# Tails of the first two batches at other places among the loads and last in the kv sums, loads of later batches behind the q transpositions

## The chip, the cores and the metric

The kernel runs on one NeuronCore of a Trainium2 chip. The metric is the device time of one execution in microseconds (us), as the median of several runs. The engines are TensorE (PE, with its weight loads shown apart as PEld), VectorE (DVE), ScalarE (ACT), GpSimd (POOL) and SyncE (SP), which issues nearly all DMAs of this kernel on one queue.

## The reference

Attention with linear cost, followed by a feed-forward layer. All inputs and the output are float32; 8 batches, 8 heads, 576 positions, head dimension 64.

```python
theta = pi / 2 * arange(S) / S
phi(x) = concat([max(x, 0) * cos(theta), max(x, 0) * sin(theta)], axis=-1)   # 64 -> 128 features
q_p, k_p = phi(q), phi(k)
kv  = einsum('bhsf,bhsd->bhfd', k_p, v)
z   = sum(k_p, axis=s)
num = einsum('bhsf,bhfd->bhsd', q_p, kv)
den = einsum('bhsf,bhf->bhs', q_p, z) + 1e-6
x   = (num / den) as [4608, 512]          # rows: batch and position, columns: head and dimension
h   = x @ w_in                            # 512 -> 2048
out = max(0.01 * h, h) @ w_out            # 2048 -> 512
```

## The kernel before

**Tiling.** The 576 positions of a batch are 512 "main" positions (four tiles j = 0 to 3 of 128) and a tail of 64. The tails of two heads share one 128-row tile, so a batch's k tail (`kpt`, four weights of 128 x 128) covers all its heads; each of the k and v tails is loaded in two DMAs of 64 KB with rows of 256 bytes (`load_kvtail`, L91). The main part of q, k or v of a batch is 1 MB with rows of 1 KB (`load_main`, L81), as one DMA or as two halves of four heads. The q tails of all batches form a ninth group of 512 rows at the end. Groups 0 to 7 are the batches, group 8 is the tails.

**Steps of a batch.** DVE (in part ACT) builds `kpm` and `kpt` from k (`k_main`, L236, two instructions for one tile j, a cosine and a sine half; `k_tail`, L243). v is cast to float16 into `vmain` and `vtail` (`v_main`, `v_tail`; on POOL from batch 4 on). `kv_mm` (L256) sums k by v over all positions into PSUM: for each pair of heads one tail matmul of 132 columns, which opens the sum, and then eight main matmuls of 66 columns. Two of the columns are ones, so that z comes with kv. `q_prep` (L294) builds `qp`, again two DVE instructions for one tile; it is transposed on PE (`q_transpose`, batches 0 and 1) or by DMA (`q_transpose_dma`, L302). `num` (L328) multiplies it by kv and `divide` (L342) gives x, which is transposed too. `ffn1` (L402) and `ffn2` (L421) are the feed-forward layer: 64 matmuls of 512 columns each for one group.

**Order.** The schedule is manual: every engine takes its instructions in the order in which the program emits them, and waits in that order. The first two batches are written out by hand. For the others the matmuls of ffn1 of group g+1 and ffn2 of group g are woven into a list of units with positions (16 positions for one group), and each of the other steps has a position at which it is emitted (`weave`, L546; `load_steps`, `kv_steps`, `q_steps`, `out_steps`). For the same position, the order of the calls decides. `q_steps(b, start, step, lag)` emits the preparation of tile j at `start + j * step` and its transposition by DMA at `lag` behind it; `load_steps(b, pk, pv, pq)` gives the positions of the loads of k, of v (each with its tail) and of q. SP's queue takes loads, transpositions by DMA and the stores of `out` in one order.

**Buffers.** All 1 MB loads use a pool of seven `stage` buffers in turn, the tails of k and v one of four. PSUM has two buffers for ffn1, two for ffn2 and one for kv sums and num.

**The start.** Loads stand in this order before: q of batch 0 in two halves, the tails of k and v, then first half of k, first half of v, second halves; then w_in in eight pieces. Behind them: w_out pieces 0 and 1, q of batch 1, tails of batch 1, w_out pieces 2 and 3, halves of k and v of batch 1, and then batch 2. Dummy matmuls (`idle`, L159) fill PE's time while it waits for the first loads.

Of the kernel before, what the change touches and what calls it, by code (L numbers as in the profile page):

```python
# [14 lines left out]
J = 4  # L15
# [3 lines left out]
def kernel(  # L19
# [14 lines left out]
    nc = tc.nc  # L34
# [11 lines left out]
    NE = D + 2  # L46
# [25 lines left out]
    def psum(where, shape, dtype, name):  # L72
        p = {"h": ps_h, "o": ps_o, "n": ps_n}[where]
        return p.tile(shape, dtype, name=name, tag="ps_" + where)

    st = {}
    ACT, DVE, POOL = nc.scalar, nc.vector, nc.gpsimd
# [3 lines left out]
    def load_main(nm, src, b, parts=(0, 1)):  # L81

        if parts[0] == 0:
            st[nm, b] = stage.tile([P, H, J, D], dt.float32, name=f"{nm}st", tag="stage")
        lo, hi = 4 * parts[0], 4 * parts[-1] + 4
        nc.sync.dma_start(  # L86
            st[nm, b][:, lo:hi],
            src[b, lo:hi, 0:MAIN, :].rearrange("h (p j) d -> p h j d", j=J),
        )

    def load_kvtail(nm, src, b):  # L91

        t = kvtail.tile([P, H // 2, D], dt.float32, name=f"{nm}tl", tag="kvtail")
        v4 = src[b, :, MAIN:S, :].rearrange("(c o) p d -> o p c d", o=2)
        for o in range(2):
            nc.sync.dma_start(t[o * TAIL : (o + 1) * TAIL], v4[o])  # L96
        st[nm + "t", b] = t
# [18 lines left out]
    def load_halves(b):  # L116
        for hg in range(2):
            load_main("k", k, b, (hg,))
            load_main("v", v, b, (hg,))
# [20 lines left out]
    def load_w2(i):  # L140
        t = stage.tile([P, 4, DM], dt.float32, name="w2st", tag="stage")
        nc.sync.dma_start(t, w2v[i])
        st["w2", i] = t

    load_main("q", q, 0, (0,))
    load_main("q", q, 0, (1,))
    load_kvtail("k", k, 0)
    load_kvtail("v", v, 0)
    load_halves(0)
    for i in range(NB):  # L150
        for cp in range(2):
            load_w1(i, cp)
# [6 lines left out]
    def idle(n):  # L159
        ps = psum("o", [P, MAIN], dt.float32, "ps_idle")  # L160
        for _ in range(n):
            nc.tensor.matmul(ps, lhsT=blank[:, 0:P], rhs=blank)  # L162
# [18 lines left out]
        base=0,  # L181
# [3 lines left out]
    for o in range(2):  # L185
# [3 lines left out]
            base=MAIN,  # L189
# [12 lines left out]
    vmain, vtail = [], []  # L202
# [15 lines left out]
    def phi_half(eng, o, i, col):  # L218
        if eng is ACT:
            nc.scalar.activation(o, i, AF.Relu, scale=col)  # L220
        else:
            eng.tensor_scalar(  # L222
                out=o, in0=i, scalar1=0.0, scalar2=col, op0=ALU.max, op1=ALU.mult
            )
# [7 lines left out]
    def kp_tiles(b):  # L232
        st["kpm", b] = kppool.tile([P, H, J, F], dt.float16, name="kpm")
        st["kpt", b] = kppool.tile([P, H // 2, F], dt.float16, name="kpt")

    def k_main(b, j, eng_c, eng_s, lo=0, hi=H):  # L236
        kpm, kst = st["kpm", b], st["k", b]
        for eng, t, f in ((eng_c, cos_t, 0), (eng_s, sin_t, D)):
            phi_half(
                eng, kpm[:, lo:hi, j, f : f + D], kst[:, lo:hi, j, :], t[:, j : j + 1]  # L240
            )

    def k_tail(b, eng_c, eng_s):  # L243
        kpt, kt, c = st["kpt", b], st["kt", b], J
        phi_half(eng_c, kpt[:, :, 0:D], kt, cos_t[:, c : c + 1])
        phi_half(eng_s, kpt[:, :, D:F], kt, sin_t[:, c : c + 1])

    def v_main(b, lo, hi, eng):
        copy(eng, vmain[b % 2][:, lo:hi, :, 0:D], st["v", b][:, lo:hi])

    def v_tail(b, eng):
        for o in range(2):
            sl = slice(o * TAIL, (o + 1) * TAIL)
            copy(eng, vtail[b % 2][sl, :, o, 0:D], st["vt", b][sl])

    def kv_mm(b, hg, ps):  # L256
        kpm, kpt = st["kpm", b], st["kpt", b]
        for cc in range(2):
            c = 2 * hg + cc
            nc.tensor.matmul(  # L260
                ps[:, 2 * cc * NE : 2 * (cc + 1) * NE],
                lhsT=kpt[:, c, :],
                rhs=vtail[b % 2][:, c].rearrange("p a e -> p (a e)"),
                start=True,
                stop=False,
            )
            for o in range(2):
                h = 2 * c + o
                for j in range(J):
                    nc.tensor.matmul(  # L270
                        ps[:, (2 * cc + o) * NE : (2 * cc + o + 1) * NE],
                        lhsT=kpm[:, h, j, :],
                        rhs=vmain[b % 2][:, h, j, :],
                        start=False,
                        stop=(o == 1 and j == J - 1),
                    )

    def kv_all(b):
        ps = psum("n", [P, 2, 512], dt.float32, "ps_kv")[:, :, 0 : 4 * NE]
        for hg in range(2):  # L280
            kv_mm(b, hg, ps[:, hg])
        nc.scalar.copy(kv[b].rearrange("p (a h) e -> p a (h e)", a=2), ps)

    def kv_half(b, hg, where):
        ps = psum(where, [P, 4 * NE], dt.float32, "ps_kvh")
        kv_mm(b, hg, ps)
        nc.scalar.copy(kv[b][:, 4 * hg : 4 * hg + 4].rearrange("p h e -> p (h e)"), ps)
# [201 lines left out]
    for j in range(J):  # L489
# [2 lines left out]
        q_transpose(0, j, ACT)  # L492
        idle(1)
    kp_tiles(0)
    k_tail(0, DVE, DVE)
    v_tail(0, DVE)
    for j in range(J):
        k_main(0, j, DVE, DVE, 0, 4)
    v_main(0, 0, 4, ACT)
    for j in range(2):  # L500
        k_main(0, j, ACT, DVE, 4, 8)
# [29 lines left out]
    for m in range(4):  # L531
        ffn1(0, m, half, MAIN, range(2, 4))

    for i in range(2):
        load_w2(i)
    load_main("q", q, 1)
    load_kvtail("k", k, 1)
    load_kvtail("v", v, 1)
    for i in range(2, 4):
        load_w2(i)  # L540
    load_halves(1)
# [21 lines left out]
    def at(pos, f, *args):  # L563
        steps.append((pos, lambda: f(*args)))
# [16 lines left out]
    ps = psum("n", [P, 2, DM], dt.float32, "ps_o")  # L581
# [27 lines left out]
    ps = psum("n", [P, 2, MAIN], dt.float16, "ps_x")  # L609
# [41 lines left out]
    def load_steps(b, pk, pv, pq):  # L651
        at(pk, load_k, b)
        at(pv, load_v, b)
        at(pq, load_main, "q", q, b)

    def out_steps(b, start, step, lag):
        for j in range(J):
            at(start + j * step, num, b, j)
            at(start + j * step + lag, x_transpose_dma, b, j)

    def q_steps(b, start, step, lag):
        for j in range(J):
            at(start + j * step, q_prep, b, j)
            at(start + j * step + lag, q_transpose_dma, b, j)
# [9 lines left out]
    kv_steps(3, 20, 0.7, 24, ACT)  # L674
    out_steps(3, 24.5, 1.4, 1)

    load_steps(4, 20.5, 22.5, 19)
    kv_steps(4, 28, 1.2, 34, POOL)
    q_steps(4, 30, 1, 0.8)
    out_steps(4, 36.8, 2, 1.6)  # L680

    for b in range(5, NG):
        base = 16 * (b - 2)
        if b < B:
            load_steps(b, base - 14.5, base - 13, base - 17)
            kv_steps(b, base - 9.5, 1.4, base - 2, POOL)
        else:
            for j in range(J):
                at(base - 11.5 + 2 * j, load_qtail, j)
        q_steps(b, base - 8, 2, 1)  # L690
        out_steps(b, base + 1, 2, 1.6)
# [32 lines left out]
```

## Time and profile before

| | |
|---|---|
| median of 3 runs | 296.37 us (295.9 to 296.65) |
| the profiled execution | 297.1 us, of which the span from the first to the last instruction is 295.0 us |
| granted TensorE clock | 1.000 |
| PE busy | 286.8 us (97%), 1932 matmuls |
| DVE busy | 132.9 us (45%) |
| ACT busy | 107.8 us (37%) |
| POOL busy | 24.0 us (8%) |
| DMA | 56.93 MB, 88773 packets, of them 56880 under 512 bytes; mean 193 GB/s |
| chain that ended last | PE 80%, DMA 13%, SP's queue 3%, ACT 1% |

Times in the profile are us from the span's start. Matmuls overlap in the records: one of 512 columns is shown with 0.38 us and the next one starts 0.216 us behind it. A bracket at the end of a timeline's row gives how long the engine was idle before it and what ended that. "Chain" is the work that ended last, followed back from the last instruction to whatever released it at each step. The state of a queue is not shown as such: what a DMA waits for is read from its issue by SP, and from the first instruction that uses what it loads.

### The profile page before, as it was taken

How to read it: one execution, taken by the hardware profiler on the slowest of the kernel's cores; microseconds unless marked ns; L12 is line 12 of the kernel's file. 1: busy time of each engine (PE TensorE's matmuls, PEld its weight loads, DVE VectorE, ACT ScalarE, POOL GpSimd, SP SyncE). 2: the span in 40 equal slices, each digit the busy share in tenths (PEclk: the TensorE clock that was granted, in tenths of full speed). 3: DMA queues.
4: the chain of work that ended last, by engine and by line, in shares of the span. 5: the costliest groups of instructions: out<-in, count | busy, mean ns of one | idle time of the engine just before them, and what ended most of it. 6: DMA issues, size and time to landing. Idle time of an engine off the chain costs nothing.

```text
span 295.0 us, 4811 instructions
## 1 busy us (share of the span) xinstructions
PE 286.8 (97%) x1932; PEld 153.9 (52%) x1932; DVE 132.9 (45%) x328; ACT 107.8 (37%) x128; POOL 24.0 (8%) x36
## 2 busy tenths in 40 slices
PE   8799999999999999999999999999999999999995
PEld 3575556465455455555545554555445544444444
DVE  6950578934855925933572347333323211000011
ACT  4846376664253422242223222322222232222200
POOL 2055000000000400400300021000000000000000
PEclk9999999999999999999999999999999999999999
DMA  7999999999999999999978995416681210011132
GB/s 219 355 386 406 290 350 346 329 170 333 186 269 285 205 248 265 267 158 315 241 143 230 216 234 126 110 53 144 143 159 56 71 53 38 36 43 61 41 71 71
DMA packets 88773, 56.93 MB, mean 193 GB/s; under 512 B 56880, under 2 KB 81712, under 8 KB 88240
## 3 DMA queue, kind: packets, MB, share of 16 engines
q1 hardware_dynamic: 88672, 56.57, 75.7%
q8 instruction: 15, 0.25, 0.4%
q14 instruction: 6, 0.05, 0.1%
q10 hardware_dynamic: 80, 0.07, 0.1%
HBM read 36.70 MB, written 9.44 MB: 156 GB/s over the span
## 4 chain that ended last, share of the span: by engine, by line
PE 80%; DMA 13%; SPq 3%; ACT 1%; issue 0%; DVE 0%; POOL 0%
PE ps_h L411 37%; PE ps_o L430 37%; DMA ktl<-in_k_dram 5%; DMA w1st<-in_moe_w_in_dram 4%; DMA vst<-in_v_dram 3%; PE ps_num L333 3%; PE ps_kv L270 2%; SPq L86 2%; SPq L96 1%; SPq L138 1%; DMA out_dram<-osb 1%; PE ps_kv L260 0%; ACT xT L389 0%; ACT g L419 0%; ACT xT L612 0%
## 5 line engine op out<-in xcount | busy, mean ns | idle before, releaser
L411 PE MATMUL ps_h<-xT,w 128*128 128x512 f16 (+1 forms) x592 | 143.1, 373 | 0.6 <-ACT g L419 0.2
L430 PE MATMUL ps_o<-w,g 128*128 128x512 f16 x560 | 139.4, 379 | 0.0
L419 ACT ACTIVATE g<-ps_h 128x1024 f16<-128x1024 f32 x72 | 73.5, 1024 | 141.7 <-PE ps_h L411 141.6
L411 PEld LDWEIGHTS <-w 128*128 128x128 f16 x592 | 64.3, 114 | 53.6 <-issue 1.3
L430 PEld LDWEIGHTS <-g 128*128 128x128 f16 x560 | 54.1, 98 | 61.6 <-issue 0.2
L230 DVE COPY osb<-ps_o 128x512 f32<-128x512 f32 x33 | 22.7, 690 | 76.6 <-PE ps_o L430 76.6
L344 DVE TENSOR_SCALAR den<-ps_num 128x8 f32<-128x8 f32 x28 | 4.6, 166 | 54.1 <-PE ps_num L333 54.1
L230 POOL CAST vmain<-vst 128x1024 f16<-128x1024 f32 (+1 forms) x9 | 9.8, 1107 | 136.6 <-DMA vst<-in_v_dram 136.6
L349 DVE TENSOR_TENSOR xs<-ps_num,rden 128x512 f16<-128x512 f32 x28 | 19.4, 691 | 1.0
L222 DVE TENSOR_SCALAR kpm<-kst,sin_t 128x512 f16<-128x512 f32 (+1 forms) x40 | 18.3, 472 | 0.7 <-DMA kst<-in_k_dram 0.7
L222 DVE TENSOR_SCALAR qp<-qst,cos_t 128x512 f16<-128x512 f32 (+1 forms) x34 | 16.3, 479 | 3.8 <-DMA qst<-in_q_dram 3.8
L222 DVE TENSOR_SCALAR qp<-qst,sin_t 128x512 f16<-128x512 f32 (+1 forms) x34 | 16.1, 472 | 0.0
L333 PEld LDWEIGHTS <-qpT 128*128 128x128 f16 (+1 forms) x256 | 11.2, 101 | 7.3 <-issue 1.9
L222 DVE TENSOR_SCALAR kpm<-kst,cos_t 128x512 f16<-128x512 f32 (+1 forms) x29 | 14.1, 485 | 0.1
L333 PE MATMUL ps_num<-kv,qpT 128*128 128x66 f16 (+1 forms) x256 | 12.4, 194 | 0.0
L270 PEld LDWEIGHTS <-kpm 128*128 128x128 f16 x256 | 10.6, 97 | 2.8 <-DVE kpm L222 0.7
L162 PE MATMUL ps_idle<-blank 128*128 128x512 f16 x28 | 9.2, 467 | 1.2 <-DVE blank L157 1.2
L228 ACT COPY qpT<-ps_qt 128x1024 f16<-128x1024 f16 x8 | 7.8, 1019 | 7.0 <-PE ps_qt L323 7.0
L230 DVE CAST w<-w2st 128x2048 f16<-128x2048 f32 x4 | 4.9, 1227 | 11.7 <-DMA w2st<-in_moe_w_out_dram 11.7
L230 POOL CAST w<-w1st 128x1024 f16<-128x1024 f32 x8 | 8.3, 1042 | 16.4 <-DMA w1st<-in_moe_w_in_dram 16.4
L270 PE MATMUL ps_kv<-vmain,kpm 128*128 128x66 f16 x192 | 8.1, 193 | 0.0
L348 DVE RECIPROCAL rden<-den 128x8 f32<-128x8 f32 x36 | 7.3, 203 | 1.2
(57 smaller groups left out, 102.6 us busy)
## 6 DMA issues: line engine op xcount, KB each, us to landing
out_dram<-osb SPq DMA_DIRECT2D x32, 256.0 KB, 2.7
qst<-in_q_dram SPq DMA_DIRECT2D x7, 1024.0 KB, 8.0
kst<-in_k_dram SPq DMA_DIRECT2D x6, 1024.0 KB, 7.9
vst<-in_v_dram SPq DMA_DIRECT2D x6, 1024.0 KB, 8.3
w1st<-in_moe_w_in_dram SPq DMA_DIRECT2D x8, 512.0 KB, 12.1
w2st<-in_moe_w_out_dram SPq DMA_DIRECT2D x4, 1024.0 KB, 11.3
kst<-in_k_dram SPq DMA_DIRECT2D x4, 512.0 KB, 8.2
vst<-in_v_dram SPq DMA_DIRECT2D x4, 512.0 KB, 8.6
```

What stands on the lines that cost most here:

```text
L86: nc.sync.dma_start(st[nm, b][:, lo:hi], src[b, lo:hi, 0:MAIN, :].rearrange("h (p j) d -> p h j d", j=J),)
L162: nc.tensor.matmul(ps, lhsT=blank[:, 0:P], rhs=blank)
L222: eng.tensor_scalar(out=o, in0=i, scalar1=0.0, scalar2=col, op0=ALU.max, op1=ALU.mult)
L228: nc.scalar.copy(o, i)
L230: eng.tensor_copy(o, i)
L270: nc.tensor.matmul(ps[:, (2 * cc + o) * NE : (2 * cc + o + 1) * NE], lhsT=kpm[:, h, j, :], rhs=vmain[b % 2][:, h, j, :], start=False, stop ...
L333: nc.tensor.matmul(ps[lo:hi, h // 4, (h % 4) * NE : (h % 4 + 1) * NE], lhsT=qpT[:, h, lo:hi], rhs=kv[b][:, h, :],)
L348: nc.vector.reciprocal(rden, den)
L349: nc.vector.tensor_tensor(out=xs, in0=ps[:, :, 0 : 4 * NE].rearrange("p a (b e) -> p a b e", e=NE)[:, :, :, 0:D], in1=rden.rearrange("p (a ...
L411: nc.tensor.matmul(ps[:, m % 2, lo:hi], lhsT=w1[m // 4][c // 2][:, c % 2, m % 4 : 512 : 4], rhs=xT[:, c, lo:hi], start=(c == 0 and lo == 0 ...
L419: nc.scalar.activation(st["g", g][:, m - 1 : m + 1, :], ps, AF.Lrelu)
L430: nc.tensor.matmul(ps, lhsT=st["g", g][:, m, tt * P : (tt + 1) * P], rhs=w2[:, m, :], start=(m == 0), stop=(m == NFT - 1),)
```

## The change

Five edits, none of which adds or removes an instruction:

1. In the loads of batch 0 the four tail DMAs go behind the first halves of k and v. On DVE the k tail and v tail of batch 0 go behind the four pieces of the first half of k.
2. In `kv_mm` the tail matmul comes last for each pair of heads and closes the sum, and the first main matmul opens it.
3. In the loads of batch 1 the k tail goes between w_out pieces 0 and 1 and the v tail behind piece 1, both ahead of q.
4. For batch 4, the load of q moves from position 19 to 21.3 and the load of k from 20.5 to 21.4, behind the transpositions of q of batch 3 (18.8 to 21.2). The step of `q_steps(4, ...)` goes from 1 to 0.8, which puts the preparations at 30, 30.8, 31.6 and 32.4 and the transpositions at 30.8 to 33.2. The k pieces of that batch stay at 29.2, 30.4, 31.6 and 32.8.
5. For batches 5 to 7, the load of q moves from `base - 17` to `base - 14.6`, 0.1 ahead of the load of k.

```diff
     load_main("q", q, 0, (0,))
     load_main("q", q, 0, (1,))
+    load_main("k", k, 0, (0,))
+    load_main("v", v, 0, (0,))
     load_kvtail("k", k, 0)
     load_kvtail("v", v, 0)
-    load_halves(0)
+    load_main("k", k, 0, (1,))
+    load_main("v", v, 0, (1,))
...
         for cc in range(2):
             c = 2 * hg + cc
-            nc.tensor.matmul(
-                ps[:, 2 * cc * NE : 2 * (cc + 1) * NE],
-                lhsT=kpt[:, c, :],
-                rhs=vtail[b % 2][:, c].rearrange("p a e -> p (a e)"),
-                start=True,
-                stop=False,
-            )
             for o in range(2):
...
                         rhs=vmain[b % 2][:, h, j, :],
-                        start=False,
-                        stop=(o == 1 and j == J - 1),
+                        start=(o == 0 and j == 0),
+                        stop=False,
                     )
+            nc.tensor.matmul(
+                ps[:, 2 * cc * NE : 2 * (cc + 1) * NE],
+                lhsT=kpt[:, c, :],
+                rhs=vtail[b % 2][:, c].rearrange("p a e -> p (a e)"),
+                start=False,
+                stop=True,
+            )
...
     kp_tiles(0)
+    for j in range(J):
+        k_main(0, j, DVE, DVE, 0, 4)
     k_tail(0, DVE, DVE)
     v_tail(0, DVE)
-    for j in range(J):
-        k_main(0, j, DVE, DVE, 0, 4)
     v_main(0, 0, 4, ACT)
...
-    for i in range(2):
-        load_w2(i)
+    load_w2(0)
+    load_kvtail("k", k, 1)
+    load_w2(1)
+    load_kvtail("v", v, 1)
     load_main("q", q, 1)
-    load_kvtail("k", k, 1)
-    load_kvtail("v", v, 1)
     for i in range(2, 4):
         load_w2(i)
     load_halves(1)
...
-    load_steps(4, 20.5, 22.5, 19)
+    load_steps(4, 21.4, 22.5, 21.3)
     kv_steps(4, 28, 1.2, 34, POOL)
-    q_steps(4, 30, 1, 0.8)
+    q_steps(4, 30, 0.8, 0.8)
     out_steps(4, 36.8, 2, 1.6)
...
-            load_steps(b, base - 14.5, base - 13, base - 17)
+            load_steps(b, base - 14.5, base - 13, base - 14.6)
```

## The prediction

> **What bounds the kernel now.** I read the page first, then busy time by stage, then the chain of waits, then the timelines of single engines around the steps that move. The page's row of TensorE (40 slices of 7.4 us) is full but for its ends:
> ```profile
> PE   8799999999999999999999999999999999999995
> ```
> Busy time by stage (first column the stage, then its length, then PE busy with the count) makes it exact: from 60 to 281 us PE is busy 221.00 of 221.00 us.
> ```profile
> 0.00:60.00 60.00, 55.42 (x437) 32.28 (x438) 40.25 (x114) 36.62 (x52) 11.01 (x20) 1.00 1.02 331
> 60.00:281.00 221.00, 221.00 (x1434) 115.54 (x1433) 90.14 (x211) 70.85 (x76) 13.02 (x16) 1.00 0.72 163
> ```
> So what moves after 60 us cannot gain; it can only open a hole. Before 60 us DMA is the bound (share 1.02). The chain runs through the loads there and reaches PE by the second half of v of batch 1 (start, length, what):
> ```profile
> 37.26 10.15 DMA vst<-in_v_dram
> ...
> 48.13 0.58 PE ps_kvh L270 x8
> ```
> PE's timeline shows where it waits for loads and where it does not:
> ```profile
> 36.48 0.61 PE L323 MATMUL ps_qt<-ident,qp 128*128 128x128 f16 x8
> ...
> 44.40 0.22 PE L260 MATMUL ps_kvh<-vtail,kpt 128*128 128x132 f16 x1
> 44.90 0.41 PE L270 MATMUL ps_kvh<-vmain,kpm 128*128 128x66 f16 x8 [0.28 <-DVE vmain L230]
> ...
> 47.70 0.22 PE L260 MATMUL ps_kvh<-vtail,kpt 128*128 128x132 f16 x1
> 48.13 0.58 PE L270 MATMUL ps_kvh<-vmain,kpm 128*128 128x66 f16 x8 [0.21 <-POOL vmain L230]
> ```
> The tail matmul is through in 0.06 us (in the chain), so PE loses 0.44 us at 44.46 and 0.37 us at 47.76, with 0.17 us more among the matmuls behind: 0.98 us in all. This is what batch 1 can give.
>
> Last, the sums of batch 4 (DVE's timeline, then PE's):
> ```profile
> 97.55 1.26 DVE L222 TENSOR_SCALAR kpm<-kst,cos_t 128x512 f16<-128x512 f32 x1
> 98.73 1.25 DVE L222 TENSOR_SCALAR kpm<-kst,sin_t 128x512 f16<-128x512 f32 x1
> ...
> 102.96 0.48 DVE L222 TENSOR_SCALAR kpm<-kst,sin_t 128x512 f16<-128x512 f32 x1
> 103.36 0.48 DVE L222 TENSOR_SCALAR qp<-qst,cos_t 128x512 f16<-128x512 f32 x1
> 103.75 0.48 DVE L222 TENSOR_SCALAR qp<-qst,sin_t 128x512 f16<-128x512 f32 x1
> ```
> ```profile
> 103.36 0.22 PE L260 MATMUL ps_kv<-vtail,kpt 128*128 128x132 f16 x1
> 103.42 0.42 PE L270 MATMUL ps_kv<-vmain,kpm 128*128 128x66 f16 x8
> ```
> DVE works from 94.92 to 104.83 without a gap. The last piece of kpm of batch 4 (j=3, the sine at 102.96) ends at 103.44; PE needs it at its fourth main matmul, 103.42 + 3 x 0.032 = 103.52. The kernel before has no slack there.
>
> **The change, part by part.** Profiled execution: 297.1 us, span 295.0 and 2.1 around it; the median of the runs, 296.37, is 0.73 below. I work out the difference and add it to the median.
>
> *Tails of batch 0 behind the first halves of k and v.* The same 3.25 MB stand ahead of the end of v. SP issues the four tails in 2.75 us (1.79 to 4.54) and k only at 4.58; DMA falls from 383 GB/s (4 to 5 us) to 277 and 229 (5 to 7 us) and is back at 339. Afterwards 2 MB are queued first. If all that shortage were saved: (383-277 + 383-229)/383 = 0.68 us; but small packets are a part of it, and an engine still at the second half of q does not starve. Bounds -0.68 and +0.2 (tails late); I take 0, nearest to the unchanged bytes. DVE has the same pieces in another order: its last q piece begins at 8.43, so k starts at 8.83 whether or not it landed earlier; eight pieces at 0.265, two of the k tail and two casts of the v tail at 0.30 end near 12.1, as now (12.18). The matmuls wait for ACT's cast of v until 12.05 anyway. Nothing.
>
> *Tail matmul last.* Same 24 + 8 kinds of matmuls. Where PE waits for v (48.13), the first tail's 0.06 us now lies behind the wait: +0.06. Elsewhere 0.
>
> *Tails of batch 1 between the w2 loads, ahead of q.* DVE's first q piece starts at 34.91, as q lands. Behind it the tails land at 35.37, 35.8, 36.2 and 36.5 (issues plus times to landing): 1.6 us for four. Put ahead of q, they make it land near 36.5. The first qp is then ready at 36.5 + 0.40 + 0.48 = 37.4 instead of 35.79. PE reaches this transposition at 36.48, so 0.69 of the 1.6 us was slack and PE waits 0.9. The w2 casts follow on DVE (the third would end at 41.0, PE needs it near 42). But k and v land as before, since the same bytes stand ahead of them: PE comes 0.9 us later to waits of 0.98. Net 0, between -0.4 (tails at 0.28 each, as the 1.1 us of the first batch) and +0.4 (0.45 each, and DVE's casts late). The front's 64 KB pieces show what the rate may be; the Trainium skill has another. "DMA: Bandwidth & Descriptors", section Bandwidth, measures 0.95 us for 64 KB (another queue). By it four take 3.8 us, PE waits 3.1, and the sum is 2.1 us higher; the 1.6 us of this trace decide.
>
> *Loads of batch 4 behind the transpositions of batch 3.* SP's order was transposition, q, out, two transpositions, k, transposition, v (75.00 to 90.80). Transpositions come first now, then q, k and tails together, then v. Batch 6 has q and k adjacent already: issues at 131.59 and 132.25, DVE takes the tail and k without a wait. From SP free near 83.3, that pattern (q to v 6.5 us, less the transposition of 2.9 in it) issues v near 87 and lands it near 96.4 instead of 97.0. The q pieces are wanted at 96.76, the tail at 93.72. No cost.
>
> *q steps of batch 4 at 0.8.* DVE's order was k0 q0 k1 q1 k2 q2 k3 q3. At 32.4 q3 now precedes k3 at 32.8. Two pieces at a spacing of 0.395 go ahead of k3: 0.79 us. PE, queued at the sums with all the feed-forward matmuls behind, waits 0.79 + 0.06 (mains start earlier by the tail) = 0.85 us, and nothing after 60 us gives it back. Bounds: 0 (DVE's stretch of 1.26 us beside POOL's cast gone) and 1.0.
>
> *q of batches 5 to 7 just ahead of k.* k of batch 5 now stands behind q (6 us for the pair, as at 131.59), but issues near 107 instead of 108.55, with no transposition behind a load. DVE already waits for this tail:
> ```profile
> 115.33 0.35 DVE L222 TENSOR_SCALAR kpt<-ktl,cos_t 128x256 f16<-128x256 f32 x1 [2.67 <-DMA ktl<-in_k_dram]
> ```
> Behind it are the division of num 4/1 and all k pieces to 126.2. I put the landing at 115.0 to 116.1, 0.8 later at most; PE comes 0.85 later itself. So 0, bounds 0 and +1.5. Batch 6 does not change its order on SP; batch 7's tail lands near 172 instead of 169.9 against 171.62: nothing.
>
> Sum: 0 + 0.06 + 0 + 0 + 0.85 + 0 = +0.91; 296.37 + 0.91 = **297.3**. A run of this kernel tells about 0.3% (0.89 us) from no change, so this stands on the border.
>
> **Rivals.**
> - *The stream of loads closes its holes (faster).* DMA ran at 294, 166 and 239 GB/s from 31 to 34 us and at 307 and 205 from 35 to 37, against 380: (86+214+141+73+175)/380 = 1.8 us, just where q's rows and the four tails meet. Among 8 KB rows the tails may cost less. If q lands by 35.8 as well and v 1 us earlier, the 0.98 us go. With 0.68 in front: 297.3 - 0.98 - 0.68 = 295.6; with the front alone 296.6. For it: the holes. Against: the landings have no holes; w2, k and v follow at 2.3 to 2.6 us per MB and 1.5 us per half, so the slowest engine was never idle. It decides where v lands before 46.5.
> - *Tail of batch 5 late (slower).* Each 1 us beyond 116.2 holds DVE, num 4/2 (PE at 117.21, its psum free at 116.99) and the sums at 126.36. At 2 us more than I give it: 298.3 to 299.
> - *q of batch 1 later than 36.5.* Against it: the tails' own 1.6 us. If PE waits 1.6: +0.6, 297.9.
> - *POOL's casts move, and the stall with them.* DVE's two k pieces beside POOL's casts took 1.26 and 1.25 us instead of 0.48: spacing 1.18 for 0.395, so 1.57 lost. Had v landed by 94, that is over before DVE's run, and 0.85 vanishes: 296.4. The rows put v at 96.4, so it is unlikely. The Trainium skill, "SBUF — State Buffer", section "Who interferes with whom", says that whichever of the two starts first blocks the other for its whole instruction. The trace agrees for DVE (its pieces end 0.28 us after POOL's).
>
> **How the numbers follow.** Forecast 0.42 (own range 296.9 to 297.6; 0.24 slower, 0.18 within); closed holes 0.25 (0.11 faster, 0.14 within); late tail 0.15 (slower); late q 0.10 (0.09 slower, 0.01 within); casts moved 0.08 (0.02 faster, with a little of the holes, 0.06 within). Together: faster 0.13, same 0.39, slower 0.48. The range leaves out the best of the holes and the worst of the late tail: 295.6 to 298.5.
>
> **What would show it.** PE waits some 0.9 us before the fourth main matmul of batch 4's sums, for DVE kpm; some 0.9 before the first transposition of batch 1, for DVE qp; none at the two sums of batch 1; v's second half lands within 0.5 us of 47.4. The forecast is wrong if batch 4 shows no wait, if v lands before 46.5, or if PE waits for num or xT after 105 us.

## The result, and the profile after

The changed kernel takes 298.77 us (median of 9 runs, 297.29 to 300.48), the kernel before 296.65 (9 runs beside them, 295.9 to 297.26). The ratio is 1.0086, with a 95% interval from 1.0057 to 1.0115: slower by 0.6 to 1.2%. The forecast of 297.3 was 1.5 us too low, and the median lies 0.3 us above the range. The profiled execution took 298.7 us with a span of 296.6, 1.6 us more than before. Medians, ranges and ratios, here and below, leave out three runs in a slow state: one of c_q4 (302.77 us), one of f_bcopy (1709.47) and one of the kernel before (774.07, beside e_mm and the three runs whose names begin with f).

First the page: the row of the granted clock (40 slices). Then busy time by stage (stage, length, PE, PEld, DVE, ACT and POOL busy, clock, DMA share, GB/s).
```profile
PEclk9989999999999999999999999999999999999999
```
```profile
0.00:60.00 60.00, 54.70 (x432) 32.48 (x433) 39.52 (x111) 35.31 (x51) 11.01 (x20) 0.97 1.04 331
60.00:281.00 221.00, 220.67 (x1432) 115.49 (x1431) 92.18 (x213) 71.80 (x77) 12.38 (x16) 1.00 0.68 162
14.00:16.00 2.00, 1.59 (x18) 1.13 (x18) 1.93 (x8) 0.98 (x3) 0.00 (x0) 0.53 1.05 387
16.00:18.00 2.00, 1.98 (x24) 1.48 (x23) 1.15 (x4) 0.21 (x1) 1.68 (x2) 0.62 1.05 386
```
Two things show. From 60 to 281 us PE is no longer wholly busy: 0.33 us is missing. And from 14 to 18 us the clock is 0.53 and 0.62, where before it was 1.00.

The chain of waits tells where the first 40 us went (start, length, what):
```profile
6.10 7.01 DMA kst<-in_k_dram
...
13.19 0.91 ACT kpm L223 x2
14.10 0.27 ACT kv L290
14.41 1.04 PE ps_numh L371 x16
15.45 1.28 PE ps_idle L165 x3
...
21.91 12.11 PE ps_h L414 x64
34.02 4.32 PE ps_o L433 x20
38.34 0.45 PE ps_qt L326 x8
```
The second half of k of batch 0 lands at 13.11 (before: 12.61). ACT's casts wait for it, the copy of the first sums is queued behind these casts, and the first numerator matmuls wait for the copy. Before, the corresponding row stood at 13.92:
```profile
13.92 0.67 PE L368 MATMUL ps_numh<-kv,qpT 128*128 128x66 f16 x16 [0.82 <-ACT kv L287]
```
After, the 16 matmuls start at 14.41 and take 1.04 us instead of 0.67, at half clock. PE then reaches the first transposition of batch 1 at 38.17 instead of 36.48, without a wait there, because it is later itself than q, which landed at 36.98 (before 34.88):
```profile
38.17 0.61 PE L326 MATMUL ps_qt<-ident,qp 128*128 128x128 f16 x8
...
46.00 0.42 PE L266 MATMUL ps_kvh<-vmain,kpm 128*128 128x66 f16 x8
46.26 0.22 PE L273 MATMUL ps_kvh<-vtail,kpt 128*128 128x132 f16 x1
```
The sums of batch 1 start at 46.00 with no waiting time worth naming (44.40 and 0.98 us of waits before). At 57.5 us the kernel is 1.06 us behind. The rest is lost at the sums of batch 4, in DVE's timeline and in PE's:
```profile
103.29 0.47 DVE L225 TENSOR_SCALAR qp<-qst,cos_t 128x512 f16<-128x512 f32 x1
103.68 0.48 DVE L225 TENSOR_SCALAR qp<-qst,sin_t 128x512 f16<-128x512 f32 x1
104.08 0.47 DVE L225 TENSOR_SCALAR kpm<-kst,cos_t 128x512 f16<-128x512 f32 x1
104.47 0.47 DVE L225 TENSOR_SCALAR kpm<-kst,sin_t 128x512 f16<-128x512 f32 x1
```
```profile
104.41 0.26 PE L266 MATMUL ps_kv<-vmain,kpm 128*128 128x66 f16 x3
105.00 0.33 PE L266 MATMUL ps_kv<-vmain,kpm 128*128 128x66 f16 x5 [0.33 <-DVE kpm L225]
```
q3 stands ahead of k3 on DVE, as forecast, and the fourth main matmul starts 0.49 us after its turn (105.00 - 104.41 - 3 x 0.032). From here to the end nothing changes: 1.06 + 0.49 = 1.55 of the 1.6 us.

### The profile page after: what moved, and what is told of

Its sections match the earlier page's. It is cut to its first block, busy times and chain, and to the rows that moved or that the text cites. A ratio compares the mean times of both kernels' runs of the same rounds, so it can differ in the third digit from the quotient of the medians.

```text
span 296.6 us, 4813 instructions
## 1 busy us (share of the span) xinstructions
PE 287.3 (97%) x1932; PEld 154.7 (52%) x1932; DVE 134.2 (45%) x328; ACT 107.5 (36%) x128; POOL 23.4 (8%) x36
## 4 chain that ended last, share of the span: by engine, by line
PE 88%; DVE 3%; DMA 3%; ACT 2%; SPq 2%; issue 1%; ACTq 0%
PE ps_h L414 40%; PE ps_o L433 39%; PE ps_num L336 3%; DMA kst<-in_k_dram 2%; PE ps_kv L266 2%; DVE kpm L225 2%; DVE qp L225 1%; SPq L96 1%; PE ps_numh L371 1%; DMA out_dram<-osb 1%; PE ps_kvh L266 1%; SPq L86 1%; PE ps_qt L326 1%; ACT xT L392 1%; PE ps_kv L273 0%
## 5 line engine op out<-in xcount | busy, mean ns | idle before, releaser
L225 DVE TENSOR_SCALAR qp<-qst,sin_t 128x512 f16<-128x512 f32 (+1 forms) x34 | 16.7, 490 | 0.0
L266 PEld LDWEIGHTS <-kpm 128*128 128x128 f16 x256 | 11.4, 100 | 4.1 <-DVE kpt L225 0.9
```

What stands on the lines that cost most here:

```text
L225: eng.tensor_scalar(out=o, in0=i, scalar1=0.0, scalar2=col, op0=ALU.max, op1=ALU.mult)
L266: nc.tensor.matmul(ps[:, (2 * cc + o) * NE : (2 * cc + o + 1) * NE], lhsT=kpm[:, h, j, :], rhs=vmain[b % 2][:, h, j, :], start=(o == 0 and ...
```

## The experiments

Each median is that of runs beside runs of the kernel before; the ratio to these (it is not that of the medians) stands with its 95% interval. "The stall" below is the time by which the fourth main matmul of batch 4's sums starts after its turn.

### The parts alone

**a_front**: edits 1 and 2, the order of batch 0 and the tail matmul last.
```diff
+    load_main("k", k, 0, (0,))
+    load_main("v", v, 0, (0,))
     load_kvtail("k", k, 0)
     load_kvtail("v", v, 0)
-    load_halves(0)
+    load_main("k", k, 0, (1,))
+    load_main("v", v, 0, (1,))
... (DVE's order and kv_mm as in the change)
```


> Edits 1 and 2 alone: tails of batch 0 behind the first halves of k and v, tail matmul last; all else as before. Theory (front): the second half of k of batch 0 lands some 0.5 us later (13.1 instead of 12.6 us) and TensorE has less to do from 10.7 to 14.1 us, so the granted clock falls to half for 3.4 us in most runs; the first x of batch 0 comes 1 to 1.9 us later, of which batch 1's waits of 0.98 us take back up to 0.98: total +0.3 to +1.5 us, mean clock 0.994 where it fell. Rival (chance): whether the clock falls depends only on the phase of the run, so runs of before show it as often, and this kernel stays within 0.3 us. Rival (prediction as it stood): +0.06 us, clock 1.000.

Measured 298.33 (296.91 to 300.64), 1.0053 [1.0025, 1.0080]. The part that I had put at nothing costs most of the loss. The profiled execution, 297.06, is one of its fastest, and even there k's second half lands at 13.05 and the numerators come late (PE's timeline):
```profile
14.35 0.67 PE L371 MATMUL ps_numh<-kv,qpT 128*128 128x66 f16 x16 [1.27 <-ACT kv L290]
```
In 4 of 12 runs the clock was 0.992 to 0.994, in the others 1.0. The spread is wide: 3.7 us.

**b_batch1**: edit 3.
```diff
-    for i in range(2):
-        load_w2(i)
+    load_w2(0)
+    load_kvtail("k", k, 1)
+    load_w2(1)
+    load_kvtail("v", v, 1)
     load_main("q", q, 1)
-    load_kvtail("k", k, 1)
-    load_kvtail("v", v, 1)
```


> Edit 3 alone: tails of batch 1 between the pieces of w_out and ahead of q. Theory (late q): q of batch 1 lands at 36.5 to 37.0 instead of 34.9 us, TensorE waits 0.9 to 1.5 us for qp ahead of the first transposition, and the waits of 0.98 us at the two sums of batch 1 are gone: total 0 to +0.5 us. Rival (holes close): v lands before 46.5 us and the total falls by 0.4 to 1 us. Theory (front) expects no change of its own here and a clock of 1.000.

Measured 296.71 (295.87 to 299.06), 0.9998 [0.9975, 1.0021]. The net of nothing is right, but not by the way that was expected: q landed at 35.23, not at 36.5 to 37.0, and PE waited 0.28 us for it, not 0.9 to 1.5. v's second half landed at 46.42, which was to be the sign that the holes close; it says nothing, because e_mm and f_bcopy, without edit 3, have 46.14 and 46.04.

**c_q4**: the spacing of the q steps of batch 4.
```diff
-    q_steps(4, 30, 1, 0.8)
+    q_steps(4, 30, 0.8, 0.8)
```


> The step of q_steps(4) alone, 0.8 instead of 1; loads as before. Theory (k behind q): the last kpm piece of batch 4 comes two DVE pieces (0.79 us) later and TensorE waits 0.85 us at the fourth main matmul of its sums: +0.8 us. With the changed loads the wait was 0.50 us in the profile of the whole change, because POOL's casts started 1.6 us earlier against DVE's work; here they should start as before, so the wait is the full one. Rival (no cost): the wait is hidden, total within 0.2 us.

Measured 297.74 (296.78 to 299.67), 1.0043 [1.0016, 1.0070]. In PE's timeline the stall is 103.46 - 102.59 - 3 x 0.032 = 0.77 us:
```profile
102.59 0.26 PE L270 MATMUL ps_kv<-vmain,kpm 128*128 128x66 f16 x3
103.46 0.33 PE L270 MATMUL ps_kv<-vmain,kpm 128*128 128x66 f16 x5 [0.62 <-DVE kpm L222]
```

**d_loads**: the load positions of edits 4 and 5, without the q steps.
```diff
-    load_steps(4, 20.5, 22.5, 19)
+    load_steps(4, 21.4, 22.5, 21.3)
...
-            load_steps(b, base - 14.5, base - 13, base - 17)
+            load_steps(b, base - 14.5, base - 13, base - 14.6)
```


> The loads of batches 4 to 7 at their new positions alone (k and q of batch 4 behind the transpositions of batch 3, q of batches 5 to 7 just ahead of k); step of q_steps(4) 1 as before. Theory (k behind q) and prediction: no wait of TensorE after 60 us, total within 0.2 us; POOL's casts for batch 4 start about 0.5 us earlier, DVE's last kpm piece ends by 103.5 us. Rival (late tail): the k tail of batch 5 lands later than 116.2 us, DVE is held and TensorE waits for num or the sums of batch 5: +0.5 to +2 us.

Measured 296.39 (295.93 to 297.29), 0.9985 [0.9966, 1.0003]; no new wait (PE is busy for 221.00 us from 60 to 281 us). The four parts' ratios add up to 0.53 + 0 + 0.43 - 0.15 = 0.8%, the whole is 0.86%.

**e_mm**: edit 2 alone, all else as before.
```diff
-            nc.tensor.matmul(..., lhsT=kpt[:, c, :], ..., start=True, stop=False)
             for o in range(2):
...
+            nc.tensor.matmul(..., lhsT=kpt[:, c, :], ..., start=False, stop=True)
```

> The kernel before with only the tail matmul put last in every pair of the kv sums; loads and VectorE order as before. Theory of the front (the load order of batch 0 is what costs): nothing, 296.4 to 296.8, since the tails are ready long before the main halves and PE does the same matmuls. Rival (the tail matmul last is what costs in the two edits of the front): 297.5 or more, with PE waiting 0.3 us or more before tail matmuls at the sums of some batch.

Measured 296.75 (296.12 to 298.15), 1.0013 [0.9995, 1.0030]. It is the order of batch 0, not the tail matmul.

### The clock, and the queue on ScalarE

**f_copy**: the changed kernel, with the first sums and their copy ahead of ACT's casts of k's second half.
```diff
-    for j in range(2):
-        k_main(0, j, ACT, DVE, 4, 8)
     idle(6)
     kv_half(0, 0, "o")
+    for j in range(2):
+        k_main(0, j, ACT, DVE, 4, 8)
```


> The changed kernel, with one more edit: the first sums of batch 0 and the copy of them on ScalarE are written ahead of ScalarE's two casts of k's second half, so that the copy no longer queues behind casts that wait for that half. Theory of the late half (k's second half lands 0.5 to 0.7 us later behind the tails, ScalarE's casts wait for it, and the copy of the first sums waits behind them): the first numerator matmuls start at about 13.2 us instead of 14.4, and the median falls by 0.5 to 1.2 us, to 297.5 to 298.2. Theory of the clock (the gap of TensorE before the first numerator matmuls lets the granted clock fall to half for 3.4 us in many runs): the gap shrinks to about 0.4 us, the clock is 0.998 or more in every run, and the median falls by 1.2 to 1.8 us, to 297.0 to 297.5. If neither holds: 298.5 or more.

Measured 300.25 (298.66 to 301.19), 1.0120 [1.0090, 1.0151]. Both theories failed. The numerators start at 13.50 as meant, and the clock is 0.997 or more in all runs. But PE, now early, waits for q of batch 1, which landed at 37.06:
```profile
38.02 0.62 PE L326 MATMUL ps_qt<-ident,qp 128*128 128x128 f16 x8 [1.08 <-DVE qp L225]
```
So the first transposition stays about where it was in the changed kernel (38.17). The stall is 1.58 us here: POOL's casts came while DVE did k1 (1.28 and 1.25 us for 0.48), later than in the other traces. Whether the edit brings that about was not tried.

**f_idle**: the changed kernel, with the gap ahead of the first numerators filled.
```diff
-    idle(1)
+    idle(6)
     num_half(0, 0, 0, "n")
```


> The changed kernel with six dummy matmuls instead of one behind the first sums of batch 0, so that the gap of 1.2 us before the first numerator matmuls is filled with 512-column matmuls (5 x 0.213 = 1.07 us); nothing else is moved. Theory of the clock: clock 0.998 or more in every run, median down by about 1.2 us, to 297.3 to 297.8, the first numerator matmuls still at about 14.4 us. Theory of the late half: the runs at clock 1.0 are as slow as before, median 298.2 to 298.8.

Measured 299.44 (297.84 to 301.13), 1.0092 [1.0064, 1.0120]. The clock is 0.998 or more in all runs, and the time does not fall; it lies above what either theory allowed. PE waits at the same place, for q that landed at 37.47:
```profile
38.44 0.62 PE L326 MATMUL ps_qt<-ident,qp 128*128 128x128 f16 x8 [1.36 <-DVE qp L225]
```
The half clock is real, but where the clock holds, the late loads take its place.

**f_bcopy**: the kernel before with the edit of f_copy (the same diff, against the kernel before).

> The kernel before with the edit of f_copy alone (first sums and their copy ahead of ScalarE's two casts of k's second half). In the trace of before the first numerator matmuls start at 13.92 and wait for the copy, which waits behind those casts for k's second half. Theory of the late half: they start at about 13.3, but the second sums still wait for v's second half (14.10, cast done at 14.74) against 15.07 now, so the gain is at most 0.3 to 0.5 us: 296.0 to 296.4. If that queue is not what sets the start: no change, 296.5, with the start at 13.9.

Measured 296.52 (295.77 to 298.94), 1.0005 [0.9987, 1.0023]. The numerators start at 13.28, and it brings nothing that can be told. Nor is that start much earlier: b_batch1, e_mm and g_nofront, whose batch 0 has the loads in the old order and no such edit, have 13.40, 13.49 and 13.43. The 13.92 of the trace before was a late one.

### One part undone

**g_nob1**: the changed kernel without edit 3.
```diff
 (against the changed kernel)
-    load_w2(0)
-    load_kvtail("k", k, 1)
-    load_w2(1)
-    load_kvtail("v", v, 1)
+    for i in range(2):
+        load_w2(i)
     load_main("q", q, 1)
+    load_kvtail("k", k, 1)
+    load_kvtail("v", v, 1)
```


> The changed kernel with the batch-1 part undone: q of batch 1 ahead of the tails of batch 1 again, the rest as changed. Theory of the load stream (the tails of batch 0 between the halves make every later load 0.9 us later, the tails of batch 1 ahead of q add to that, and q of batch 1, landing at 37.0 to 37.5, sets the first transposition of batch 1 at 38.0 to 38.4): q lands at 34.3 to 35.3, the first transposition starts at 36.7 to 37.3, and the median falls by 0.7 to 1.2 us, to 297.6 to 298.1. Rival, the parts add up: the batch-1 part alone measured 0, so undoing it changes nothing, 298.5 to 299.0.

Measured 298.55 (297.51 to 300.76), 1.0076 [1.0048, 1.0104]: no gain, as the rival said. With q ahead of the tails it lands at 35.55 and the first transposition is at 36.60, but the 1.4 us come back at the next load, k and v of batch 1 (its k lands at 43.29):
```profile
45.40 0.41 PE L266 MATMUL ps_kvh<-vmain,kpm 128*128 128x66 f16 x8 [0.42 <-DVE vmain L233]
```
So it is not q alone that sets the time, but the stream. (The trace of g_nob1 has the full clock, that of the changed kernel has not, so the 36.60 is not q's doing alone.)

**g_nofront**: the changed kernel with batch 0's loads and DVE order as before.
```diff
 (against the changed kernel)
-    load_main("k", k, 0, (0,))
-    load_main("v", v, 0, (0,))
     load_kvtail("k", k, 0)
     load_kvtail("v", v, 0)
-    load_main("k", k, 0, (1,))
-    load_main("v", v, 0, (1,))
+    load_halves(0)
... (DVE's order as before)
```


> The changed kernel with the load and VectorE order of batch 0 as before; the tail matmul last, the batch-1 part and the later parts as changed. Theory of the load stream: k's second half lands at 11.8 to 12.6 instead of 13.1, q of batch 1 at 35.2 to 36.2, the first transposition starts at 36.2 to 37.0 instead of 38.0 to 38.4, only the stall at the fourth main matmul of batch 4's sums (0.5 to 0.8 us) is left: 297.0 to 297.8. Rival, the parts add up: 296.5 + 1.7 for the q steps as c_q4 measured + 0: 298.0 to 298.4.

Measured 297.41 (296.90 to 297.79), 1.0019 [1.0004, 1.0034]. Without edit 1 the kernel does what the prediction said of the rest, in numbers. q lands at 35.83 and PE waits 0.85 us; the stall is 103.97 - 103.04 - 3 x 0.032 = 0.83 us:
```profile
36.80 0.62 PE L323 MATMUL ps_qt<-ident,qp 128*128 128x128 f16 x8 [0.85 <-DVE qp L222]
...
103.04 0.26 PE L263 MATMUL ps_kv<-vmain,kpm 128*128 128x66 f16 x3
103.97 0.33 PE L263 MATMUL ps_kv<-vmain,kpm 128*128 128x66 f16 x5 [0.67 <-DVE kpm L222]
```
Edit 1 thus costs 298.77 - 297.41 = 1.4 us by the medians, 2.0 us by the ratios (0.67% of 296.7). The 1.7 us that the rival takes from c_q4 are 1.2 by the median given above.

**g_noq4**: the changed kernel without the new spacing.
```diff
 (against the changed kernel)
-    q_steps(4, 30, 0.8, 0.8)
+    q_steps(4, 30, 1, 0.8)
```

> The changed kernel with only the spacing of the q steps of batch 4 put back to 1. Both theories: the wait before the fourth main matmul of batch 4's sums goes, and the median falls by 0.5 to 1.3 us, to 297.5 to 298.2; the first transposition of batch 1 stays at 38.0 to 38.4. If the stall is made up for later anyway (the chain takes the 0.5 us back): 298.6 or more.

Measured 299.44 (298.22 to 299.99), 1.0084 [1.0061, 1.0108]. A miss: the median lies where it was to lie if the stall were made up for anyway. But the trace says otherwise: the stall is gone, and from the start of batch 4's sums to the end it takes 191.7 us instead of 192.1. In this trace the front was the worst of all (k's second half at 14.10). That the spread which edit 1 brings, about 2 us, hides a gain of 0.4 is argued, not shown.

**h_frontidle**: a_front with `idle(6)` for `idle(1)` (the diff of f_idle, against a_front).

> The kernel of a_front (order of batch 0 and tail matmul last, nothing else) with six dummy matmuls instead of one before the first numerator matmuls, so that TensorE's gap of 1.4 us is filled. In a_front 4 of 12 runs had a granted clock of 0.992 to 0.994. Theory of the clock: no run falls below 0.997 and the median falls by 0.5 to 1.2 us, to 297.1 to 297.8. Theory of the load stream: the clock holds, but the runs at full clock stay where those of a_front were (median 298.1), 297.9 to 298.5, because k's second half and what comes behind it still land 0.9 us later.

Measured 298.13 (296.71 to 300.99), 1.0054 [1.0027, 1.0081]. One run of 12 had a low clock (0.992), and the median is that of a_front less 0.2 us, as the theory of the load stream had it.

**h_frontcopy**: a_front with the edit of f_copy (the same diff, against a_front).

> The kernel of a_front with the first sums of batch 0 and their copy on ScalarE ahead of its two casts of k's second half. If the late half reaches TensorE through that queue: the first numerator matmuls start at about 13.4 instead of 14.35, the gap in which the clock fell is gone, no run below 0.997, median 297.0 to 297.7. If the second sums, which wait for v's second half at 14.6, set the pace anyway: 297.8 to 298.5.

Measured 298.74 (298.16 to 300.75), 1.0088 [1.0056, 1.0120]. The numerators start at 13.13, and PE waits at 43.21 for the last w_out piece and at 45.51 for batch 1's casts. One of 6 runs had a clock of 0.994, and both forecasts were too low. Once more the stream.

### What makes the stream late

The views print only the time at which a whole load has landed. The trace also holds the time at which each of the sixteen parts of a load completes. I took the middle and the last of them (us), for k of batch 0:

| kernel | first half, middle / last | second half, middle / last |
|---|---|---|
| before | 8.44 / 8.95 | 11.58 / 12.61 |
| f_bcopy | 8.41 / 8.76 | 11.49 / 11.77 |
| g_nofront | 8.62 / 8.96 | 11.69 / 12.12 |
| a_front | 7.26 / 8.31 | 12.04 / 13.05 |
| after | 7.33 / 8.37 | 11.99 / 13.11 |
| h_frontidle | 7.26 / 9.59 | 11.97 / 13.95 |
| g_noq4 | 7.28 / 9.87 | 11.99 / 14.10 |
| j_mid | 7.28 / 8.84 | 11.83 / 13.02 |
| j_notail | 7.19 / 8.49 | 10.61 / 11.40 |
| k_bigpack | 7.31 / 9.63 | 11.96 / 13.69 |

In the eight traces with the tails first (before, b_batch1, c_q4, d_loads, e_mm, f_bcopy, g_nofront, k_best) the last part of the first half comes 0.34 to 0.69 us behind the middle one. In the eight with edit 1 (a_front, after, f_copy, f_idle, g_nob1, g_noq4, h_frontidle, h_frontcopy) it comes 0.68 to 2.59 us behind, and a few of the sixteen parts make up that lag (in a_front 13 are through by 7.38 and three come at 8.00, 8.09 and 8.31). That lag stays with the loads that follow, up to w_in. The middle part of the second half moves by only 0.4 us on the average (11.6 to 12.0); its last part, by which the load counts as landed, comes at 11.8 to 12.6 with the tails first and at 12.6 to 14.1 with edit 1. At batch 1's first half of k the last parts are at 42.2 and 43.6 on the average: 1.4 us, as much as edit 1 costs by the medians (the groups also differ in edits 3 to 5 and in ACT's order). In 19 traces (all but j_acttail), the time of the profiled execution less the stall is 254.2 to 255.7 us more than this landing, which itself runs from 40.73 (j_notail) to 44.84 (g_noq4): where the stream is late, so is the kernel.

This bears out the Trainium skill, "DMA: Bandwidth & Descriptors", section "Why a DMA increments its semaphore by 16 and not by 1": a transfer is spread over up to 16 engines that finish independently, and only the last one makes it complete. Here the last came up to 2.6 us behind the middle.

Two readings limit the part that the lag of k's first half has in this. Between the two profiled executions of the result, k's second half comes 0.41 us later by its middle part and 0.50 by its last, because the last part of before was itself 1.03 us behind; the greater lag shows in the averages, not in this pair. And the lag has another source, which the old order has too. The trace's records of DMA packets hold an instruction fetch of 16 KB between 16.9 and 20.0 us in these 19 traces. At that time the last part of a w_in piece falls back in before from 1.09 to 2.56 us behind the middle one, in after from 1.18 to 2.67, in a_front only from 1.01 to 1.27. That the fetch does it, and that the loads lose where it meets a part that is late already, is argued.

The lag also reaches the loads that are still to be issued. SP's timeline, before and after:
```profile
6.33 0.51 SPq L86 DMA_DIRECT2D vst<-in_v_dram  x1
6.88 8.74 SPq L138 DMA_DIRECT2D w1st<-in_moe_w_in_dram  x8
```
```profile
6.76 2.04 SPq L86 DMA_DIRECT2D vst<-in_v_dram  x1
8.85 7.28 SPq L138 DMA_DIRECT2D w1st<-in_moe_w_in_dram  x8
```
The issue of v's second half takes 2.04 us instead of 0.51 (1.74 to 3.33 in the eight traces with edit 1) and ends some 0.4 us behind the landing of k's first half. Behind it, the program lets only eight loads be under way: the trace shows eight completion semaphores (counters that tell when a load has landed) used in turn, and each issue from the ninth to the sixteenth load waits for the load eight places ahead, that is for its last part. Before, the first four w_in pieces wait for tails, which landed by 7.29; the second is issued at 7.74. With edit 1 the first two wait for the first halves of k and v, and the second is issued 0.01 to 0.02 us behind the landing of v's (10.60 behind 10.58 in after, 11.58 behind 11.56 in g_noq4). In g_noq4 and h_frontidle, where the lag is greatest, the stream falls to 219 to 272 GB/s from 15 to 17 us; a_front has 389 to 393 there, and k_bigpack, with a lag nearly as great, 375 to 379. No run changed these places by themselves, so what they cost is open.

**j_notail**: a_front without the tail loads of batch 0.
```diff
 (against a_front)
+        if b == 0:
+            nc.gpsimd.memset(t, 0.0)
-        for o in range(2):
+        for o in range(2 if b else 0):
             nc.sync.dma_start(...)
```


> The kernel of a_front without the four 64 KB loads of batch 0's tails: their tiles are filled with zeros by GpSimd at the start, so the tails of k and v of batch 0 are left out of its sums. Theory of the small packets (the tails, 256 B a packet, hold the stream below 260 GB/s for two to three us when they come between the halves): k's second half lands at 10.9 to 11.6, at least 1.5 us ahead of a_front's 13.05, the first numerator matmuls start by 12.9, and the median is 295.0 to 296.2. Rival (the order of the halves and of VectorE's work is what delays): k's second half lands at 12.3 to 13.0 and the median is 297.5 to 298.3.

Measured 296.09 (295.64 to 296.72), 0.9977 [0.9957, 0.9996]. k's second half lands at 11.40, as this theory had it, and the numerators start at 13.12. Leaving the four tails out gains 0.6 us on the kernel before (296.72 beside it) and 2.2 us on a_front (298.33). The order of the halves and DVE's order are those of a_front, so neither is slow by itself.

**j_mid**: the tails between the first half of k and the first half of v; DVE's order and `kv_mm` as in a_front.
```diff
 (against a_front)
     load_main("k", k, 0, (0,))
-    load_main("v", v, 0, (0,))
     load_kvtail("k", k, 0)
     load_kvtail("v", v, 0)
+    load_main("v", v, 0, (0,))
     load_main("k", k, 0, (1,))
```


> Tails of batch 0 behind k's first half, ahead of v's first half; VectorE's order and the tail matmul as in a_front; nothing else changed. Theory of the small packets, by degrees: k's second half lands between the two orders, 12.4 to 13.1, median 296.9 to 297.9. If only tails directly ahead of k's second half delay it: 11.8 to 12.4, as before, and 296.4 to 296.9. Rival of the halves' order: as a_front, 298.0 to 298.5.

Measured 297.08 (296.52 to 297.40), 1.0016 [1.0006, 1.0027]: between the two orders, as forecast for a price by degrees. The second half of k lands at 13.02, though, about where that of a_front does (13.05).

**k_bigpack**: a_front whose tail loads read contiguous rows.
```diff
 (against a_front)
-            nc.sync.dma_start(t[o * TAIL : (o + 1) * TAIL], v4[o])
+            nc.sync.dma_start(
+                t[o * TAIL : (o + 1) * TAIL],
+                src[b, o, 0 : 4 * TAIL, :].rearrange("(p j) d -> p j d", j=4) if b == 0 else v4[o],
+            )
```


> The kernel of a_front whose four tail loads of batch 0 read, in the same places of the order and with the same 64 KB, contiguous rows of the main part (1 KB a packet instead of 256 B), so batch 0's sums use other rows than the true tails. Theory of the small packets: k's second half lands at 11.7 to 12.3 (j_notail's 11.40 and 0.6 for 256 KB at 390 GB/s), and the median is 295.9 to 296.7. Rival, four more loads between the halves cost that whatever their packets: 12.6 or later and 297.7 to 298.5, as a_front.

Measured 298.53 (296.75 to 300.59), 1.0052 [1.0022, 1.0083]: as a_front. The theory of the small packets falls: the same four loads with packets of 1 KB cost the same. The DMA view says the same (GB/s in 40 slices from 4 to 16 us; first a_front, then k_bigpack):
```profile
GB/s 372 389 375 287 229 246 300 328 355 365 382 372 376 340 291 236 203 218 158 222 264 270 295 287 352 341 341 358 348 369 358 382 375 406 348 423 348 423 348 423
```
```profile
GB/s 382 386 382 331 236 259 280 304 321 345 304 328 362 352 324 345 253 249 236 253 249 277 304 311 270 324 324 358 352 365 365 379 376 393 369 393 376 382 389 362
```
In both the stream is low from 9 to 11 us (slices 16 to 24); the large packets only make the trough a little less deep. It fits that four loads take four of the eight places whatever their packets, but that was not tested by itself.

**j_acttail**: the kernel before, with batch 0's tails issued by ACT behind its set-up.
```diff
-    load_kvtail("k", k, 0)
-    load_kvtail("v", v, 0)
     load_halves(0)
...
     nc.scalar.activation(warm, zero, AF.Lrelu)
+    load_kvtail("k", k, 0)      # issued by nc.scalar for batch 0
+    load_kvtail("v", v, 0)
```


> The kernel before with the four loads of batch 0's tails issued by ScalarE, behind its set-up activations, instead of SyncE; all else, VectorE's order too, as before. SyncE's queue gets k's first half 2.8 us sooner. If the SP queue's issue times matter: k's second half lands 0.3 to 0.8 us ahead of the kernel before (12.2 over its traces), 295.7 to 296.3. If the stream's bytes and packets set it alone: no change in the landing, 296.3 to 296.8; and if the tails then land behind 8.8 us, VectorE waits for them at the head of its queue and the kernel is slower, 297 or more.

Measured 310.08 (309.91 to 311.49), 1.0470 [1.0447, 1.0494]: ACT's issues wait for so long that PE waits for the copies behind them (ACT's timeline; its first copy stood at 7.30 in the trace of before):
```profile
6.04 0.61 ACTq L96 DMA_DIRECT2D ktl<-in_k_dram  x1
8.81 4.07 ACTq L96 DMA_DIRECT2D vtl<-in_v_dram  x2
12.92 1.93 ACT L228 COPY qpT<-ps_qt 128x1024 f16<-128x1024 f16 x2 [7.96 <-DMA ktl<-in_k_dram]
```
Each issue itself takes 0.6 us. Those of the v tail are made at 8.81 and 12.28, when k's first and second half have landed (8.79 and 12.26), whose semaphores they use again. The second half's 12.26 is as in the traces of the old order. The run says nothing for SP's queue.

**k_best**: the kernel before with the diffs of d_loads and f_copy together.

> The kernel before with the later loads of batches 4 to 7 as in d_loads and the first copy of batch 0 ahead of ScalarE's casts as in f_bcopy; nothing of the front, of batch 1 or of the q steps. The parts measured 0.9985 and 1.0005: if they add up 296.1 to 296.6, no difference that can be told or 0.1 to 0.2 per cent faster. If the earlier copy only moves a wait, 296.4 to 296.8.

Measured 296.35 (295.96 to 296.94), 0.9979 [0.9956, 1.0002]. It is not shown to be faster than the kernel before; against the changed kernel it is faster by 2.4 us by the medians.

## Why the prediction was wrong

**The step that failed** is the term "Tails of batch 0 behind the first halves of k and v", put at nothing with bounds of -0.68 and +0.2. It measured +1.4 us (2.0 by the ratios). The reason that I gave, "nearest to the unchanged bytes", nearly holds for the middle parts of the loads and not for their end: on the average of the traces k's second half is 0.4 us later by its middle part and 1.0 by its last. A few of the sixteen parts fall behind while k's first half follows q directly, and a load is there only when its last part is. The bound of +0.2 for late tails was too small as well: in g_noq4 and k_bigpack PE waits 0.49 and 0.28 us for the v tail. What makes parts of k's first half lag from 6 to 9 us is open. The tails' small packets are not the cause of the time (k_bigpack), nor is the clock alone (f_idle, h_frontidle). That k's first half follows q is enough for the lag: j_notail has 1.30 us of it there without any tail. But it takes the four loads behind it too for the loss: without them, and without their 0.25 MB, the kernel was not slower than before. Why the lag costs more with them was not settled; SP's rows above show one way. Nor is it shown that the spread of this lag (0.7 to 2.6 us) makes the spread of the runs with edit 1 (296.7 to 301.2 us at full clock): h_frontcopy has 0.76 and took 299.1 us, a_front has 1.05 and took 297.06. It is the lateness at batch 1 that goes with the time.

**The chain that the step missed** is on ACT. I argued that the first sums wait for the cast of v until 12.05 anyway. They did (11.93), but what the numerators wait for is the copy queued behind the casts of k's second half, and the row of 13.92 showed that. Where the copy was moved ahead, the loads of batch 1 took over (f_copy, h_frontcopy), so this chain carries the delay but does not make it.

**Batch 1.** "q lands near 36.5" was off by 0.5 us in the changed kernel (36.98) and by up to 1.8 in its variants (37.06 in f_copy, 37.47 in f_idle, 38.34 in g_noq4), because of the front; the rival of a late q came true, hidden in the profile after by PE's own lateness. Without edit 1 q landed at 35.83 and the wait was 0.85 for the forecast 0.9; with edit 3 alone it landed at 35.23 and the wait was 0.28, so that agreement is in part luck. The 0.98 us of waits that were to take it back are those of one trace, too: c_q4, e_mm, f_bcopy and k_best, with the old order there, show 0.3 to 0.8. The net of nothing is right (b_batch1; undone in g_nob1, no gain).

**The q steps of batch 4.** The order on DVE and the place of the wait are as predicted. The forecast was 0.85 us; the stall is 0.77 alone, 0.83 in g_nofront, 0.82 in g_nob1, 0.91 in f_idle, 1.58 in f_copy, and 0.49 in the profile after, where POOL's casts lay earlier and met other DVE pieces. c_q4 as a whole rose by more (0.43%, 1.3 us), but the interval, 0.5 to 2.1, holds the stall.

**The rest.** The tail matmul last, at 0.06, and the loads of batches 4 to 7, at nothing, are right (1.0013 and 0.9985, both with 1 in the interval). The late tail of batch 5 did not come: it landed at 115.25 and 115.67. The holes in the load stream from 31 to 37 us are gone after (331 to 436 GB/s, where before had 166 to 409), but smaller ones stand from 26 to 31 us (244 at the least), and v landed at 48.06, not before 46.5: nothing was gained by it. With edit 1 at nothing the sum is 297.3, and g_nofront, without edit 1, measured 297.41.

## What to carry to other kernels

A load has landed when the slowest of its parts has. Where the start of a kernel is bound by loads, an order with the same bytes is not a neutral order; look up when the first consumer of each late half starts, and try the order by itself before it is put at nothing. Look up too which earlier load each issue waits for: four small loads can hold half of the places. Follow also what is queued behind the instruction that waits for a load: here a copy that had its data was held by casts that had not. And where several bounds lie close together (ACT's queue, the clock, q, k of the next batch), freeing one shows the next and gains nothing.

## What the runs showed of the hardware

- Sixteen parts of a load drift apart (last against middle 0.3 to 2.6 us at k's first half, up to 3.3 near 30 us), and the drift stays with the loads behind it.
- The clock went to half without an idle window. In the trace after it is 0.50 from 14.1 to 17.5 us; in the 3.4 us ahead, PE was busy for 1.75 us:
```profile
10.70:14.10 3.40, 1.75 (x22) 0.94 (x21) 2.26 (x9) 2.08 (x5) 0.00 (x0) 1.00 1.09 351
14.10:17.50 3.40, 3.09 (x36) 2.26 (x36) 2.98 (x10) 0.88 (x3) 1.18 (x2) 0.50 1.05 386
```
 The Trainium skill, "TensorE: Matmul & The Clock Gate", section "What's actually happening", has the gate close after an idle window of about 3.4 us and says that the window runs free. The length agrees (3.41 us); here a window that was half busy was enough, and in g_noq4 and k_bigpack, whose clock fell at 14.67 and 14.85, one with 1.18 and 1.17 of 3.41 us busy. It is not always enough: a_front's trace has 1.62 us of 3.4 busy from 10.7 to 14.1 and kept 1.00, as it may where the window runs free. The mean clock was 0.992 to 0.994 in 6 of 9 runs after and 4 of 12 of a_front.
- The issue of a load can hold the engine that makes it: SP's issue of v's second half took 0.51 us before and 3.33 in g_noq4, where the lag was greatest. (The 4.07 us of ACT in j_acttail are not that; its issues took 0.6 us each and waited for the semaphores of earlier loads.)
